# Rounding keys and queries on GpSimd instead of ScalarE from the fourth attention stage on

## The chip, the cores and the metric

The kernel runs on one core of one Trainium2 chip. The metric is the time of one execution on the device in microseconds (us). The engines are TensorE (PE in the rows; PEld is its weight load), VectorE (DVE), ScalarE (ACT), GpSimd (POOL) and SyncE (SP), which issues all the DMAs here. Each engine works through its own queue in order.

## The reference

Attention over 4 batches, 8 heads, 576 positions and 64 dimensions per head, where each query keeps its 32 highest scores; then a mixture of 8 experts whose weights for the rows come from eight rounds of normalising over rows and columns. All in float32.

```python
scores = scale * np.matmul(q, k.transpose(0, 1, 3, 2))
kth = np.partition(scores, -top_k, axis=-1)[..., -top_k:-top_k + 1]
scores = np.where(scores >= kth, scores, -1000000000.0)
attn = np.exp(scores - np.max(scores, axis=-1, keepdims=True))
attn = attn / (np.sum(attn, axis=-1, keepdims=True) + 1e-09)
attn_out = np.matmul(attn, v)                 # -> x, 2304 rows of 512
P = np.exp(x @ w_gate - max)
for _ in range(8):
    P /= P.sum(1, keepdims=True) + 1e-09
    P /= P.sum(0, keepdims=True) + 1e-09
    P *= N / E
for e in range(E):                            # w1: 512 x 1024, w2: 1024 x 512
    out += P[:, e:e + 1] * (np.maximum(x @ w1[e], 0.0) @ w2[e])
```

## The kernel before

**High and low parts.** The matrix products that have to be accurate are made of float32r operands: a value is split into a high part (the value rounded to float32r) and a low part (the value less its high part), and a product is the sum of high by high, high by low and low by high. Three helpers do this: `hi_act` (line 82) rounds on ScalarE, `lo_pool` (line 85) subtracts on GpSimd, `lo_dve` (line 88) subtracts on VectorE.

**Attention.** `STAGES` (line 30) lists seven stages, each one batch with one or both halves of its queries (`phases`), some of them with the last 64 rows as well (`mix`). `attend_stage` runs over the four pairs of heads `hp`; `attend_heads` (line 181) loads and splits what a pair needs. Raw keys and queries come by DMA into the tile `raw` (3 buffers), issued on SyncE. For each of the two heads the keys, 128x576, become `kh` and `kl` (lines 203 and 204); for each half the queries, 128x512, become `qs`, and for the last rows, 128x256, they become `qm` (lines 188 and 189; the low part is put in place in partitions 64 to 127). `scores` (lines 122 and 123) multiplies them on TensorE. ScalarE copies the scores out (`s`, line 128), VectorE finds the 32 highest in four rounds (lines 138 and 141), GpSimd makes a small difference `eb` (line 142), ScalarE weighs (lines 144 and 145), GpSimd adds to the sums `st` (line 171) and multiplies the weights `Et` by the reciprocals (line 175). From the third stage on the weights are turned by a DMA: ScalarE splits them into 16-bit halves (`cross`, line 158), a transposing DMA writes `turned`, and ScalarE puts the halves together into `at` (`whole`, line 165). That last step does not follow its own DMA at once: it waits in the list `turning` and is put behind a later ScalarE instruction (`land`, lines 152 and 147), so that ScalarE has other work while the DMA runs. TensorE then multiplies `at` by the values (line 247).

**The experts.** Beside the attention TensorE works on visits: for an expert and one or two seated blocks of 256 rows, the hidden layer (line 446) and the outputs (line 559). Each visit loads weights as 128x1024 tiles `wr`, which ScalarE rounds to `wh` (line 83, by `hi_act`) and GpSimd turns into `wl` (line 86, by `lo_pool`), six buffers of each. The hidden values are rounded to `hh` on ScalarE (line 514), with `hl` on VectorE (line 515); outputs go through `y` (line 567) to memory. The last four blocks are done at the end in another way (`hidden_pair`, lines 671 to 730), with no attention beside them.

**Order.** The framework plans the order on every engine when the kernel is built, from priorities and its own estimate of each instruction's time; attention has priority over the visits. Within an engine the planned order is fixed at run time, with waits where operands or buffers are not ready. `X` is the dictionary of finished or begun blocks: it has 2 entries in the first stage, 4 in the second, 6 in the third and 9 from the fourth on.

Of the kernel before, what the change touches and what calls it, by code (L numbers as in the profile page):

```python
# [51 lines left out]
def kernel(  # L52
# [11 lines left out]
    nc = tc.nc  # L64
# [16 lines left out]

    def hi_act(dst, src):
        nc.scalar.activation(dst, src, AF.Copy)  # L83

    def lo_pool(dst, src, hi):
        nc.gpsimd.tensor_tensor(dst, src, hi.bitcast(F32), op=OP.subtract)  # L86
# [27 lines left out]
    X = {}  # L114
# [64 lines left out]
    va, vb = slice(0, 64), slice(64, 128)  # L179

    def attend_heads(b, hp, phases, xts, xm):
        lo = lo_dve if (phases, b, hp) == ((0,), 0, 0) else lo_pool

        def load_q(name, o, n, bufs):
            qr = ap_.tile([128, n], F32, name="raw", bufs=RAW)
            nc.sync.dma_start(qr, q[b, hp, :, o:o + n])
            qs = ap_.tile([128, n], F32R, name=name, bufs=bufs)
            hi_act(qs, qr)
            lo(qs[64:128], qr[64:128], qs[64:128])
            return qs  # L190

        def load_phase(ph):
            return load_q("qs", ph * 512, 512, 2)

        if phases:
            qs = load_phase(phases[0])
        ks = []
        for i in range(2):
            kr = ap_.tile([128, S], F32, name="raw", bufs=RAW)
            nc.sync.dma_start(kr, k[b, 2 * hp + i])  # L200
            kh = ap_.tile([128, S], F32R, name="kh", bufs=2)
            kl = ap_.tile([128, S], F32R, name="kl", bufs=2)
            hi_act(kh, kr)
            lo(kl, kr, kh)
            ks.append((kh, kl))
        vr = values[:, hp % 2, :]
        nc.sync.dma_start(vr[:, 0:512], v[b, hp, :, 0:512])
        for i, r in enumerate((va, vb)):
            nc.sync.dma_start(vr[r, 512 + 64 * i:576 + 64 * i], v[b, hp, r, 512:576])
        for ph in phases:  # L210
            if ph != phases[0]:
                qs = load_phase(ph)
            last = ph == phases[-1] and xm is not None
            qm = load_q("qm", 1024, 256, 1) if last else None
            attend_phase(b, hp, qs, qm, ks, vr, xts[ph], xm if last else None)
        if not phases:
            attend_rest(hp, load_q("qm", 1024, 256, 1), ks, vr, xm)
# [34 lines left out]
    def attend_phase(b, hp, qs, qm, ks, vr, xt, xm):  # L252
        nq = 256 if xm is None else 320
        at = ap_.tile([128, 9, 320], F32, name="at", bufs=1)

        def put(blocks, cs, src):
            nc.scalar.activation(at[:, blocks, cs], src, AF.Copy)

        crossed = at if len(X) > 4 else None
        weight_tiles(qs, ks, put, b == 0 or crossed is not None, crossed)  # L260
        if xm is not None:
            def put_rest(rows, blocks, src):
                nc.scalar.activation(at[rows, blocks, 256:320], src, AF.Copy)
            rest_weights(qm, ks, put_rest)
        order = TAIL_FIRST if len(X) > 2 else range(5)

        def weigh():
            av = pst.tile([128, 512], F32, name="pt")
            weigh_values(av, vr, at, nq, order)
            nc.scalar.activation(xt[:, hp, :], av[:, 0:256], AF.Copy)  # L270
            if xm is not None:
                nc.scalar.activation(xm[:, hp, :], av[:, 256:320], AF.Copy)

        if turning:
            turning.append(weigh)
        else:
            weigh()
# [23 lines left out]
    def attend_rest(hp, qm, ks, vr, xm):  # L301
        at = ap_.tile([128, 9, 64], F32, name="tmp", bufs=1)

        def put(rows, blocks, src):
            nc.scalar.activation(at[rows, blocks, :], src, AF.Copy)

        rest_weights(qm, ks, put)
        av = pst.tile([128, 512], F32, name="pt")
        weigh_values(av, vr, at, 64, TAIL_FIRST)
        nc.scalar.activation(xm[:, hp, :], av[:, 0:64], AF.Copy)  # L310

    def attend_stage(b, phases, mix):
# [13 lines left out]
        for hp in range(HP):  # L326
            if (b, phases) == (0, (0,)) and hp in (1, 2):
                with tc.high_priority(offset=-BIG):
                    if hp == 1:
                        first_quarter(xts[0])  # L330
                    else:
                        ready[0] = first_half(xts[0])
            attend_heads(b, hp, phases, xts, xm)
# [45 lines left out]
    def board(blk, seat):  # L379
        pieces = BLOCKS[blk]  # L380
        step = 2 if pieces[0][0] == "t" else 1
        for t in range(0, 2, step):
            x = X[pieces[t]]
            if step == 2:
                x = bass.AP(tensor=x.tensor, offset=x.offset, ap=[list(p) for p in x.ap[:-1]] + [[1, 256]])
            cs = slice(seat.c0 + t * 128, seat.c0 + (t + step) * 128)
            for kk in range(KD):
                hi_act(seat.xh[:, kk, cs], x[:, kk, :])
                lo_dve(seat.xl[:, kk, cs], x[:, kk, :], seat.xh[:, kk, cs])
# [446 lines left out]
```

## Time and profile before

| what | us |
|---|---|
| median of 3 runs (1862.12 to 1863.7) | 1862.87 |
| profiled execution, its own time | 1861.39 |
| its span in the trace | 1859.6 |
| TensorE busy | 1794.2 |
| VectorE busy | 1208.9 |
| ScalarE busy | 1172.1 |
| GpSimd busy | 1047.8 |

How to read the rows below. A line of the stretches gives from:to, its length, then for PE, PEld, DVE, ACT and POOL the busy us and in brackets the number of instructions, then the granted clock of TensorE (1.00 is full speed), the DMA engines' busy share and GB/s. A line of the waits gives engine, line and operation, then whom it waited for: us in total, how many times, the longest. A line of a tile's instructions gives the count, then the shortest, median and longest duration in ns, then the first and last start in us, then the shape; the lines "who: us, times" under it say what ended the idle time of the engine before them. A line of the groups gives the count, then busy us and the mean ns of one, then the idle us before them and who ended it. A line in order of time gives start and duration in us, and in square brackets the idle time before it and who ended that. Matmuls overlap one another in the rows, so TensorE's busy time is not its peak.

### The profile page before, as it was taken

The page shows a single profiled execution, that of the slowest core. Times are in us where ns is not written, and L with a number is a line of the kernel's source. Part 1 is how long each engine was busy: PE and PEld are TensorE (multiplying, and loading weights), DVE is VectorE, ACT ScalarE, POOL GpSimd, SP SyncE. Part 2 cuts the span into 40 slices and gives each one's busy share as a digit, 9 for nine tenths or more (in the row PEclk, how much of TensorE's full clock was granted, in tenths as well). Part 3 has the DMA queues.
Part 4 walks back from the last instruction along what each step waited for, and adds up shares of the span by engine and source line. Part 5 has one row for each costly group of instructions (what it writes and reads, how often), then busy time and mean ns, then how long its engine had stood idle before and what let it go on. Part 6 is the DMA issues. An engine that isn't in the chain of part 4 may idle for free.

```text
span 1859.6 us, 26250 instructions
## 1 busy us (share of the span) xinstructions
PE 1794.2 (96%) x9361; PEld 1484.4 (80%) x9361; DVE 1208.9 (65%) x2235; ACT 1172.1 (63%) x1773; POOL 1047.8 (56%) x827
## 2 busy tenths in 40 slices
PE   4899998999999999999999999999999999999998
PEld 3778787878877878878877788888888888888886
DVE  8989988888888886978965231145555555533433
ACT  5888889898988987898888435433333333333331
POOL 3369755655655547565643948945554455555441
PEclk8999999999999999999999999999999999999999
DMA  4787766666556656565554337523333333311111
GB/s 128 237 286 237 218 173 186 203 169 165 165 144 167 173 135 198 155 160 162 165 134 112 105 131 227 185 85 111 117 110 117 103 102 108 97 62 59 56 35 45
DMA packets 212674, 266.17 MB, mean 143 GB/s; under 512 B 127424, under 2 KB 131648, under 8 KB 212544
## 3 DMA queue, kind: packets, MB, share of 16 engines
q1 hardware_dynamic: 212544, 264.51, 48.0%
q8 instruction: 73, 1.20, 0.3%
q14 instruction: 57, 0.47, 0.1%
HBM read 201.54 MB, written 34.60 MB: 127 GB/s over the span
## 4 chain that ended last, share of the span: by engine, by line
PE 73%; ACT 7%; DVE 6%; issue 5%; DMA 5%; POOL 4%; SPq 0%; ACTq 0%; POOLq 0%; DVEq 0%
PE p L730 19%; PE p L559 15%; PE p L446 14%; PE p L671 9%; PE pc L671 5%; DMA wr<-in_w_dram 3%; PE pt L247 3%; DVE m L138 3%; POOL wl L86 2%; PE pb L671 2%; DVE w L141 2%; PE sp L122 2%; PE sp L123 2%; ACT wh L83 1%; ACT at L165 1%
## 5 line engine op out<-in xcount | busy, mean ns | idle before, releaser
L86 POOL TENSOR_TENSOR wl<-wr,wh 128x1024 fp32r<-128x1024 f32 x280 | 675.1, 2420 | 509.9 <-ACT wh L83 500.1
L83 ACT ACTIVATE wh<-wr 128x1024 fp32r<-128x1024 f32 x280 | 295.1, 1060 | 281.9 <-PE p L671 191.6
L138 DVE MAX8 m<-w 128x8 f32<-128x576 f32 x432 | 321.8, 754 | 6.5
L446 PE MATMUL p<-xh,wh 128*128 128x256 f32 (+1 forms) x800 | 270.3, 338 | 1.5 <-DVE hl L515 1.5
L446 PE MATMUL p<-xh,wl 128*128 128x256 f32 (+1 forms) x800 | 268.4, 336 | 0.0
L446 PE MATMUL p<-xl,wh 128*128 128x256 f32 (+1 forms) x800 | 268.4, 335 | 0.0
L559 PE MATMUL p<-wh,hh 128*128 128x512 f32 x640 | 251.2, 397 | 4.7 <-ACT hh L514 4.5
L559 PE MATMUL p<-wl,hh 128*128 128x512 f32 x640 | 249.2, 392 | 0.0
L559 PE MATMUL p<-wh,hl 128*128 128x512 f32 x640 | 239.5, 391 | 0.0
L141 DVE MATCH_REPLACE8 w<-m,w 128x576 f32<-128x576 f32 x288 | 213.8, 743 | 0.0
L515 DVE SCALAR_TENSOR_TENSOR hl<-p,hh 128x512 fp32r<-128x512 f32 x160 | 109.0, 683 | 148.0 <-ACT hh L514 146.3
L730 PE MATMUL p<-wh,h2h 128*128 128x512 f32 x512 | 199.4, 389 | 1.3 <-ACT h2h L694 0.7
L730 PE MATMUL p<-wl,h2h 128*128 128x512 f32 x512 | 199.2, 389 | 0.0
L730 PE MATMUL p<-wh,h2l 128*128 128x512 f32 x512 | 196.4, 389 | 0.0
L576 DVE SCALAR_TENSOR_TENSOR acc<-p,P,acc 128x512 f32<-128x512 f32 x120 | 89.4, 749 | 160.9 <-PE p L730 160.9
L446 PEld LDWEIGHTS p<-xh,wh 128*128 128x128 f32 x800 | 152.4, 190 | 21.4 <-DVE hl L515 3.1
L446 PEld LDWEIGHTS p<-xh,wl 128*128 128x128 f32 x800 | 152.3, 190 | 15.7 <-issue 0.8
L446 PEld LDWEIGHTS p<-xl,wh 128*128 128x128 f32 x800 | 152.3, 190 | 15.5
L138 DVE MAX8 m<-s 128x8 f32<-128x576 f32 x144 | 108.2, 752 | 76.0 <-ACT s L128 75.3
L559 PEld LDWEIGHTS p<-wh,hh 128*128 128x128 f32 x640 | 120.6, 189 | 30.3 <-ACT hh L514 7.1
L559 PEld LDWEIGHTS p<-wl,hh 128*128 128x128 f32 x640 | 120.7, 189 | 23.0 <-POOL wl L86 0.2
L559 PEld LDWEIGHTS p<-wh,hl 128*128 128x128 f32 x640 | 119.8, 188 | 23.8 <-issue 0.4
(168 smaller groups left out, 3551.8 us busy)
## 6 DMA issues: line engine op xcount, KB each, us to landing
wr<-in_w_dram SPq DMA_DIRECT2D x240, 512.0 KB, 3.5
y<-y SPq DMA_DIRECT2D x160, 256.0 KB, 2.7
raw<-in_k_dram SPq DMA_DIRECT2D x56, 288.0 KB, 3.8
raw<-in_q_dram SPq DMA_DIRECT2D x32, 256.0 KB, 3.7
p<-y SPq DMA_DIRECT2D x32, 256.0 KB, 3.5
wr<-in_w_dram SPq DMA_DIRECT2D x32, 256.0 KB, 4.0
y<-p SPq DMA_DIRECT2D x32, 256.0 KB, 3.8
values<-in_v_dram SPq DMA_DIRECT2D x28, 256.0 KB, 3.1
```

Source lines behind the costliest of these rows:

```text
L83: nc.scalar.activation(dst, src, AF.Copy)
L86: nc.gpsimd.tensor_tensor(dst, src, hi.bitcast(F32), op=OP.subtract)
L122: nc.tensor.matmul(o, qc, kh[:, cs], start=(i == 0), stop=False)
L138: nc.vector.max(m8[:, u, r, :], ws[u] if r else units[u][0])
L141: nc.vector.match_replace(ws[u], m8[:, u, r, :], ws[u] if r else units[u][0], LOWEST)
L247: weighed = nc.tensor.matmul(av[r, 0:n], vr[:, o:o + 64], at[:, block, 0:n], start=(j == order[0]), stop=(j == order[-1]))
L446: nc.tensor.matmul(ps[:, fo, :], a[:, kk, fs], x[:, k0 + kk, cs], start=(i == 0), stop=(i == 3 * nk - 1))
L515: nc.vector.scalar_tensor_tensor(seat.hl[:, ft, cs], src, 0.0, seat.hh[:, ft, cs].bitcast(F32), op0=OP.max, op1=OP.subtract)
L559: nc.tensor.matmul(ps, a[:, ft, ts], m[:, ft % 2, :], start=(i == 0), stop=(i == 3 * NFT - 1))
L576: return nc.vector.scalar_tensor_tensor(ACC[t], y, g, ACC[t], op0=OP.mult, op1=OP.add)
L671: nc.tensor.matmul(ps, w[:, kk, :], x[:, kk, :], start=(fresh and i == 0), stop=(i == 5), skip_group_check=True)
L730: nc.tensor.matmul(ps, a[:, ft, ts], m[:, ft, :], start=(i == 0), stop=(i == 11))
```

## The change

A new helper `hi_pool` rounds on GpSimd with a copy. In `attend_heads` the helper for the high part is chosen by the number of entries in `X`: `hi_act` in the first three stages, `hi_pool` from the fourth stage on. It is used for `qs` and `qm` (in `load_q`) and for `kh`. Who makes the low parts, the loads, the buffers and the late putting together of the halves are the same as before. All other rounding (weights, hidden values, seated rows) stays on ScalarE.

```diff
--- before.py
+++ after.py
@@ -81,6 +81,9 @@
 
     def hi_act(dst, src):
         nc.scalar.activation(dst, src, AF.Copy)
+
+    def hi_pool(dst, src):
+        nc.gpsimd.tensor_copy(dst, src)
 
     def lo_pool(dst, src, hi):
         nc.gpsimd.tensor_tensor(dst, src, hi.bitcast(F32), op=OP.subtract)
@@ -179,13 +182,14 @@
     va, vb = slice(0, 64), slice(64, 128)
 
     def attend_heads(b, hp, phases, xts, xm):
+        hi = hi_pool if len(X) > 6 else hi_act
         lo = lo_dve if (phases, b, hp) == ((0,), 0, 0) else lo_pool
 
         def load_q(name, o, n, bufs):
             qr = ap_.tile([128, n], F32, name="raw", bufs=RAW)
             nc.sync.dma_start(qr, q[b, hp, :, o:o + n])
             qs = ap_.tile([128, n], F32R, name=name, bufs=bufs)
-            hi_act(qs, qr)
+            hi(qs, qr)
             lo(qs[64:128], qr[64:128], qs[64:128])
             return qs
 
@@ -200,7 +204,7 @@
             nc.sync.dma_start(kr, k[b, 2 * hp + i])
             kh = ap_.tile([128, S], F32R, name="kh", bufs=2)
             kl = ap_.tile([128, S], F32R, name="kl", bufs=2)
-            hi_act(kh, kr)
+            hi(kh, kr)
             lo(kl, kr, kh)
             ks.append((kh, kl))
         vr = values[:, hp % 2, :]
```

## Rows read from the trace of the kernel before

**Rows 1.** The page: busy time of the span; the chain that ended last, by engine

```profile
PE 1794.2 (96%) x9361; PEld 1484.4 (80%) x9361; DVE 1208.9 (65%) x2235; ACT 1172.1 (63%) x1773; POOL 1047.8 (56%) x827
PE 73%; ACT 7%; DVE 6%; issue 5%; DMA 5%; POOL 4%; SPq 0%; ACTq 0%; POOLq 0%; DVEq 0%
```

**Rows 2.** Stretches of the span: busy time of each engine, granted clock

```profile
263.00:300.00 37.00, 30.56 (x190) 26.17 (x189) 31.29 (x63) 32.73 (x43) 23.75 (x23) 1.00 0.67 185
300.00:340.00 40.00, 39.16 (x247) 33.12 (x248) 37.58 (x73) 36.26 (x48) 21.91 (x22) 0.92 0.60 166
340.00:420.00 80.00, 76.29 (x505) 66.61 (x504) 70.24 (x140) 72.12 (x110) 44.30 (x41) 0.98 0.69 191
420.00:690.00 270.00, 269.09 (x1418) 219.49 (x1417) 226.63 (x445) 237.09 (x347) 149.16 (x134) 1.00 0.57 155
690.00:705.00 15.00, 15.00 (x82) 11.83 (x81) 7.39 (x14) 11.28 (x21) 14.67 (x12) 1.00 0.86 244
705.00:930.00 225.00, 225.00 (x1255) 183.78 (x1254) 185.27 (x363) 193.79 (x305) 134.30 (x119) 1.00 0.59 165
930.00:1030.00 100.00, 97.84 (x529) 77.72 (x529) 59.41 (x114) 80.87 (x112) 47.34 (x41) 1.00 0.48 131
1140.00:1210.00 70.00, 69.19 (x412) 61.67 (x411) 9.55 (x14) 35.65 (x45) 63.76 (x35) 1.00 0.60 198
1210.00:1859.00 649.00, 643.49 (x2837) 531.99 (x2835) 310.60 (x429) 214.07 (x309) 307.37 (x208) 1.00 0.28 86
```

**Rows 3.** What TensorE waited for, 263.2 to 1030 us

```profile
PE pt L247 <- ACT at L165: 6.2, 1, 6.2
PE sp L122 <- ACT s L128: 3.9, 3, 1.9
PE p L559 <- ACT hh L514: 1.9, 3, 1.2
PE p L446 <- DVE hl L515: 1.1, 1, 1.1
PE pt L362 <- ACT xm L272: 1.0, 1, 1.0
```

**Rows 4.** TensorE in order of time, at its two longest waits

```profile
300.84 4.53 PE L247 MATMUL pt<-at,values 128*64 128x256 f32 x20 [6.22 <-ACT at L165]
379.00 0.40 PE L122 MATMUL sp<-kh,qs 128*128 128x288 f32 x1 [1.95 <-ACT s L128]
```

**Rows 5.** ScalarE in order of time, before those two waits

```profile
290.79 0.68 ACT L83 ACTIVATE kh<-raw 128x576 fp32r<-128x576 f32 x1
291.36 0.62 ACT L83 ACTIVATE qs<-raw 128x512 fp32r<-128x512 f32 x1
372.72 0.63 ACT L83 ACTIVATE qs<-raw 128x512 fp32r<-128x512 f32 x1 [1.67 <-DMA raw<-in_q_dram]
```

**Rows 6.** Tile raw, 263.2 to 1030 us: the roundings, then idle time by its end

```profile
L83 ACT ACTIVATE kh<-raw x32: 667/679/711, 279.9 to 922.9; 128x576 fp32r<-128x576 f32 x32
L83 ACT ACTIVATE qs<-raw x20: 613/632/656, 263.0 to 917.5; 128x512 fp32r<-128x512 f32 x20
L83 ACT ACTIVATE qm<-raw x16: 402/410/449, 271.6 to 924.0; 128x256 fp32r<-128x256 f32 x16
  ACT qs L83: 12.0, 7
  DMA raw<-in_q_dram: 4.6, 4
```

**Rows 7.** GpSimd's groups of instructions, 263.2 to 1030 us

```profile
L86 POOL TENSOR_TENSOR wl<-wr,wh 128x1024 fp32r<-128x1024 f32 x112 | 268.5, 2406 | 154.5 <-ACT wh L83 146.4 <-issue 6.0 <-PE pt L362 0.5
L175 POOL TENSOR_SCALAR Et<-Et,st 128x576 f32<-128x576 f32 x88 | 64.9, 750 | 17.2 <-DVE st L172 16.3 <-PE sp L123 0.3
L86 POOL TENSOR_TENSOR kl<-raw,kh 128x576 fp32r<-128x576 f32 x33 | 46.8, 1434 | 7.0 <-ACT kh L83 6.7
```

**Rows 8.** What ScalarE waited for, 263.2 to 1030 us

```profile
ACT halves L158 <- POOL Et L175: 19.1, 16, 3.0
```

## The prediction

> **What bounds the kernel now.** I read the page first. TensorE is busy for 1794.2 of 1859.6 us and holds 73% of the chain that ended last; ScalarE holds 7%, GpSimd 4% [rows 1]. So work taken off ScalarE is worth nothing as such. It is worth something only where TensorE stood still for ScalarE.
>
> The second view is the table of stretches [rows 2]. The roundings that move start at 263.0 us and the last starts at 924.0 us [rows 6], so the stretches from 263 to 930 us are the ones to look at. In them ScalarE is busy for 32.73 + 36.26 + 72.12 + 237.09 + 11.28 + 193.79 = 583.3 of 667 us, 87.4%, and GpSimd for 388.1 us, 58.2% (added in the same way). TensorE's idle time is 6.44 us up to 300 us, then 0.84, 3.71 and 0.91 us up to 690 us, nothing from 690 to 930 us, and 2.16 us up to 1030 us, 14.1 us together. After 1210 us it is 5.5 us, but no attention runs there, and the change has nothing to move there.
>
> The third view says who ended that idle time: ScalarE in 6.2 + 3.9 + 1.9 + 1.0 = 13.0 us, VectorE in 1.1 us, GpSimd in none [rows 3]. The clock adds to it. The mean granted share is 0.92 from 300 to 340 us, behind the longest wait of 6.22 us [rows 2, 4]. With the levels 2.4 and 1.2 GHz that is some 6.4 us at the lower one, which costs 0.08 x 40 = 3.2 us. From 340 to 420 us (0.98) it is 0.02 x 80 = 1.6 us. What ScalarE can give back from 263 us on is thus at most 13.0 + 4.8 = 17.8 us, under 1% of the time.
>
> **The change part by part.** The threshold is passed in the fourth stage (9 entries in X, against 6 in the third), so four stages change. 32 roundings of keys, 20 of queries and 16 of last rows [rows 6] leave ScalarE. They cost it 32 x 0.679 + 20 x 0.632 + 16 x 0.410 = 21.7 + 12.6 + 6.6 = 40.9 us. ScalarE goes from 583.3 to 542.4 us, 81.3% of the stretch.
>
> **What GpSimd pays.** It runs no copy in the trace of before. The nearest row is line 175, which like the copy reads one tensor: 750 ns for 128x576 [rows 7]. Scaled by columns that is 0.667 us for 512 and 0.333 us for 256, so 24.0 + 13.3 + 5.3 = 42.7 us, and GpSimd goes from 388.1 to 430.8 us, 64.6%. The upper end is line 86 with its two inputs, 1434 ns for 576: 81.6 us, 70.4%. From 1434 ns for 576 and 2406 ns for 1024 columns [rows 7] an instruction's fixed part is 1434 - 576 x 2.17 = 184 ns, and 68 of those, 12.5 us, are the lower end. I take 42.7 us, since line 175 has the same shape and number of inputs. At either end GpSimd keeps over a quarter of the stretch free, so the range of the time doesn't hang on it.
>
> A rule speaks against the change. The Trainium skill (GPSIMD Engine Reference, section 4.1, Engine selection) keeps elementwise work off GpSimd as about half as fast as VectorE with two inputs, though it calls one input roughly line rate. The rows agree on the order: 750 ns with one input, 1434 ns with two. At one column per cycle of the 1.2 GHz that the page states, an estimate for the 68 copies is 27 us. The sum would be the same.
>
> **What hides it.** A low part needs its high part, and GpSimd makes both now, so its waits for ScalarE's query and key roundings (12.0 and 7.0 us [rows 6, 7]) become its own work. The net load on GpSimd is nearer 43 - 19 = 24 us. Behind a rounding stand `wl`, `eb`, `st` and `Et`. For `wl` there is room: GpSimd waited 146.4 us for ScalarE's `wh` before it [rows 7], and TensorE's waits name GpSimd nowhere [rows 3]. The DMAs are not moved; SyncE still issues the raw loads. But `raw` is freed by the low part, later by up to one rounding (0.75 us) where GpSimd was not waiting, and the weight loads stand behind it in SyncE's queue. I cost this at 0, covered by the six weight buffers. If that cover is gone, each such rounding costs up to 0.75 us.
>
> **What the path gains.**
> 1. Ahead of the wait at 300.84 us ScalarE works without a break. Two of its instructions are roundings that move: starts 290.79 and 291.36 us, 0.57 us apart, and the second, 0.62 us less its overlap, some 0.5 us [rows 5]. Gain 1.1 of 6.2 us. What is late next is the same `at`, since the weight roundings stay, so the clock's 3.2 us stay as well.
> 2. At 372.72 us ScalarE waited 1.67 us for a query load and then rounded for 0.63 us, 2.3 us, and TensorE then waited 1.95 us for the scores' copy [rows 4, 5]. On GpSimd that DMA wait holds nobody on ScalarE. Gain 1.95 us.
> 3. The other waits for ScalarE, 13.0 - 6.2 - 1.95 = 4.9 us, I shrink as its free share grows, 12.6% to 18.7%: 4.9 x (1 - 12.6 / 18.7) = 1.6 us, an estimate.
>
> Sum: 1.1 + 1.95 + 1.6 = 4.6 us. Against the profiled execution (span 1859.6 us, own time 1861.4 us) that is 1856.8 us. The median lies 1.5 us above that execution, so the forecast is 1862.9 - 4.6 = 1858.2 us.
>
> The framework plans the order anew from 263 us on. This can shift the waits either way, and the rivals hold what it could do.
>
> **The rivals.**
> - **Covered anyway, 1862.9 us (1860 to 1866).** The planner spends ScalarE's 41 us on issuing other work earlier; TensorE meets its waits elsewhere. For it: from 420 to 930 us TensorE idles under 1 us with ScalarE at 87% [rows 2]. Against it: the second wait above is a queue order that cannot come back in that form.
> - **All of ScalarE's lateness goes, 1862.9 - 17.8 = 1845 us.** For it: 13.0 of 14.1 us name ScalarE [rows 3], and without the 6.2 us wait the clock would not fall. Against it: the chain ahead of that wait holds only 1.1 us of roundings.
> - **Slower: GpSimd's order takes ScalarE's place, 1872 us.** A copy that waits for its load or for TensorE to be done with `kh` now stands in GpSimd's queue ahead of `Et`; `halves` on ScalarE wait for `Et`, `at` waits for both, and TensorE, in order, waits for `at`. ScalarE already waited 16 times for `Et`, 19.1 us in all, 3.0 us at most [rows 8], and GpSimd is busy for 14.67 of 15 us from 690 to 705 us [rows 2]. The price of one such miss is that of the longest wait now: 6.2 + 3.2 us of clock = 9.4 us, so 1872 us, and 1882 us for two. It decides once a rounding makes `Et` later than TensorE's work in hand. Against it: GpSimd still has 35% free, and of the many `at` only one made TensorE wait [rows 3].
> - **It costs GpSimd far more than line 175 says.** This is the upper end, 70.4%, and leads to the third rival rather than to a time of its own.
>
> **How the numbers follow.** Forecast 1858.2 us (1855 to 1861): 0.36. Covered anyway: 0.24. All lateness gone: 0.14. Slower: 0.26. A measurement of this kernel can tell about 0.2%, 3.7 us, from no change, so the bounds are 1859.1 and 1866.6 us. Of the forecast's chance 0.28 lies below 1859.1 us, with 0.14 from the third case: faster 0.42. Same: 0.08 + 0.24 = 0.32. Slower: 0.26. The range goes from 1846 us (all but the full gain) to 1873 us (one miss); two misses and the lowest end are left out, some 0.18. As cases of both signs hold much of the chance: the likeliest one's own range is 1855 to 1861 us.
>
> **What would show it.** In the profile after: 68 copies on GpSimd, near 0.75, 0.67 and 0.33 us; ScalarE's busy time lower by some 41 us and GpSimd's higher by some 43 us; the waits of GpSimd for ScalarE's `kh` and `qs` gone after 263 us; no wait of ScalarE for a query load there; TensorE's idle time from 263 to 1030 us near 9 us instead of 14.1, with the granted clock after the longest wait still dipping. The prediction is wrong if TensorE shows a new wait of over 3 us for `at`, if its waits name GpSimd, or if its idle time falls below 5 us.

## The result and the profile after

The changed kernel takes 1871.93 us (median of 5 runs, 1867.23 to 1872.81) against 1862.12 us in the same comparison. The ratio is 1.0054, 95% interval [1.0041, 1.0067]: 0.5% slower, 7.6 to 12.5 us. The forecast was 1858.2 us. The time lies within the range given, the direction is wrong.

The profiled execution took 1867.23 us with a span of 1865.4 us, against 1861.39 us before, 5.8 us more. Of the page after, the busy time of the engines and the chain that ended last:

```profile
PE 1798.3 (96%) x9361; PEld 1486.3 (80%) x9361; DVE 1214.7 (65%) x2235; ACT 1141.4 (61%) x1705; POOL 1085.4 (58%) x895
PE 77%; DVE 8%; DMA 4%; POOL 4%; ACT 4%; issue 3%; SPq 0%; POOLq 0%; ACTq 0%; DVEq 0%
```

68 instructions have gone from ScalarE (1773 to 1705) and come to GpSimd (827 to 895), as meant [rows 1]. ScalarE is busy 30.7 us less, GpSimd 37.6 us more. The 68 durations that left ScalarE add up to 40.9 us, but its instructions overlap one another in the rows (starts 0.57 us apart, duration 0.68 us [rows 5]), so its busy time falls by less.

Tile `raw` after, from 255 to 1040 us: the copies on GpSimd, then idle time by its end. One copy of queries lies ahead of 263 us. Lines of the changed kernel are 3 or 4 higher than before's.

```profile
L86 POOL CAST kh<-raw x32: 664/671/701, 278.4 to 995.9; 128x576 fp32r<-128x576 f32 x32
L86 POOL CAST qs<-raw x20: 606/615/915, 256.7 to 988.6; 128x512 fp32r<-128x512 f32 x20
L86 POOL CAST qm<-raw x16: 397/407/597, 267.4 to 997.4; 128x256 fp32r<-128x256 f32 x16
  PE sp L125: 16.8, 8
  DMA raw<-in_q_dram: 8.2, 4
```

A copy on GpSimd takes what it took on ScalarE (679, 632 and 410 ns [rows 6]). The last of them starts at 997 us instead of 924 us, so the attention is later. This shows in the last of the top-k instructions on VectorE, in before and then in after (start and duration in us):

```profile
1004.65 0.76 DVE L138 MAX8 m<-w 128x8 f32<-128x576 f32 x1
```
```profile
1072.13 0.75 DVE L141 MAX8 m<-w 128x8 f32<-128x576 f32 x1
```

The stretches of [rows 2], now of after, with one more, 1030 to 1140 us:

```profile
263.00:300.00 37.00, 32.07 (x194) 27.49 (x193) 32.67 (x67) 31.36 (x38) 25.85 (x26) 0.97 0.71 205
300.00:340.00 40.00, 40.00 (x260) 34.31 (x260) 34.71 (x70) 30.38 (x45) 22.36 (x25) 0.99 0.61 159
340.00:420.00 80.00, 75.76 (x512) 65.86 (x512) 62.60 (x120) 62.88 (x93) 49.53 (x47) 0.96 0.61 181
420.00:690.00 270.00, 267.28 (x1370) 216.32 (x1370) 209.69 (x401) 218.19 (x308) 159.72 (x146) 0.99 0.55 155
...
930.00:1030.00 100.00, 99.79 (x495) 80.53 (x494) 79.28 (x152) 84.41 (x119) 60.18 (x57) 1.00 0.56 151
1030.00:1140.00 110.00, 104.22 (x621) 86.46 (x620) 55.40 (x134) 72.72 (x104) 75.41 (x57) 0.97 0.43 122
1140.00:1210.00 70.00, 68.92 (x425) 61.80 (x425) 11.63 (x24) 35.12 (x43) 63.77 (x33) 1.00 0.61 195
```

The same stretch from 1030 to 1140 us of before:

```profile
1030.00:1140.00 110.00, 109.10 (x592) 93.10 (x590) 28.73 (x85) 46.64 (x67) 82.59 (x49) 1.00 0.41 134
```

Up to 1030 us TensorE's idle time is 4.93 + 0 + 4.24 + 2.72 + 0.21 = 12.1 us, against 14.1. From 1030 to 1140 us it is 5.8 us, against 0.9. The clock is read from stretches of 10 us, here all those of after between 263 and 1210 us in which it is below 0.99:

```profile
290.00:300.00 10.00, 6.29 (x35) 5.45 (x36) 8.24 (x18) 9.29 (x10) 8.69 (x6) 0.88 0.95 315
300.00:310.00 10.00, 10.00 (x61) 7.62 (x61) 8.81 (x19) 8.22 (x14) 6.44 (x5) 0.95 0.72 171
350.00:360.00 10.00, 5.88 (x46) 3.08 (x48) 8.19 (x17) 9.94 (x16) 7.73 (x7) 0.66 0.74 251
660.00:670.00 10.00, 7.95 (x39) 5.45 (x40) 4.95 (x10) 7.46 (x12) 4.55 (x7) 0.83 0.72 189
1110.00:1120.00 10.00, 4.79 (x34) 4.51 (x33) 6.31 (x22) 0.91 (x2) 10.00 (x7) 0.84 0.09 29
1120.00:1130.00 10.00, 10.00 (x48) 8.83 (x48) 2.80 (x10) 3.55 (x4) 10.00 (x6) 0.82 0.47 154
```

What the lower of the two levels (1.2 of 2.4 GHz) takes is the missing share times the length: 1.2 + 0.5 + 3.4 + 1.7 = 6.8 us up to 1030 us, against 3.2 + 1.6 = 4.8 us before [rows 2] (5.1 us by stretches of 10 us), and 1.6 + 1.8 = 3.4 us after 1030 us, against nothing. Where the lower clock falls into a wait, both are counted, so the sums below are upper bounds.

So the balance of idle time and clock is 14.1 + 4.8 = 18.9 us before and 12.1 + 6.8 = 18.9 us after up to 1030 us: no gain. From 1030 to 1210 us it is 0.9 + 0.8 = 1.7 us before [rows 2] and 5.8 + 1.1 + 3.4 = 10.3 us after: **8.6 us lost behind the stretch that the forecast looked at**. The medians are 9.8 us apart. The profiled pair is only 5.8 us apart: its execution of after is the shortest of five, 4.7 us under their median, and by 263 us, where only one rounding had moved, it was ahead. TensorE had started 1330 instructions there against 1315 in before; at the mean pace from 263 to 1030 us, 0.18 us for one [rows 2], that is an estimated 2.7 us, so 8.6 - 2.7 = 5.9 us should be left. That stretch in before, then in after:

```profile
0.00:263.00 263.00, 219.45 (x1315) 178.92 (x1316) 242.16 (x501) 211.61 (x377) 158.63 (x151) 0.97 0.69 217
```
```profile
0.00:263.00 263.00, 221.39 (x1330) 180.49 (x1331) 243.98 (x505) 211.91 (x378) 161.72 (x154) 0.99 0.69 218
```

What TensorE waited for in after, the largest entries from 263 to 1030 us and then from 1030 to 1210 us (total, times, longest):

```profile
PE pt L251 <- ACT at L267: 4.2, 1, 4.2
PE p L450 <- DVE hl L519: 3.7, 3, 1.9
PE pt L251 <- ACT at L168: 2.6, 1, 2.6
PE sp L125 <- ACT s L131: 1.2, 1, 1.2
...
PE pt L423 <- DVE cs L421: 2.8, 1, 2.8
PE p L450 <- POOL wl L89: 2.4, 1, 2.4
PE p L563 <- ACT hh L518: 1.1, 1, 1.1
```

The two waits that the forecast named, 6.22 us at 300.84 and 1.95 us at 379.00 [rows 4], are gone. Two others have come at 354 and 662 us. Ahead of the first ScalarE works without a break from 339.38 us, with three weight roundings in front of the `at` that it starts at 350.81 us; ahead of the second it waited 3.83 us for the top-k on VectorE. Neither row has a wait for GpSimd. TensorE in order of time at these and at the two in the later stretch:

```profile
354.12 5.32 PE L251 MATMUL pt<-at,values 128*64 128x320 f32 x20 [4.24 <-ACT at L267]
...
662.05 3.85 PE L251 MATMUL pt<-at,values 128*64 128x256 f32 x20 [2.58 <-ACT at L168]
...
1116.21 0.39 PE L423 MATMUL pt<-cs,ones 128*128 128x8 f32 x2 [2.83 <-DVE cs L421]
1118.98 0.58 PE L450 MATMUL p<-xh,wl 128*128 128x256 f32 x1 [2.38 <-POOL wl L89]
```

The last two lie in what follows the attention. When all rows are there, the experts' weights for the rows are normalised in eight rounds (line 423 is one of their products), and for the blocks done at the end GpSimd prepares the **right factors**: differences of rows (tile `tf`, line 626) and low parts. GpSimd in order of time around the last wait:

```profile
1091.86 2.36 POOL L89 TENSOR_TENSOR wl<-wr,wh 128x1024 fp32r<-128x1024 f32 x1 [5.24 <-ACT wh L83]
1094.17 1.28 POOL L626 TENSOR_TENSOR tf<-xt 128x512 f32<-128x512 f32 x1
...
1115.91 0.72 POOL L626 TENSOR_TENSOR tf<-xt,tf 128x256 f32<-128x256 f32 x1
1116.59 4.67 POOL L89 TENSOR_TENSOR wl<-wr,wh 128x1024 fp32r<-128x1024 f32 x2
```

From 1094.17 to 1116.59 us, 22.4 us, GpSimd works on right factors without a `wl` between. In before the first of them starts at 1031.5 us, beside visits of two blocks, which use each weight for twice the rows. The first products of a visit of a single block start at 1085.4 us, and from 1107.6 us on there are only such visits. They take their `wl` so fast that GpSimd is busy for 63.76 of 70 us from 1140 us on [rows 2]: it has little room for the factors there.

### The profile page after: what moved, and what is told of

It is laid out like the page before. It is cut to its first block, busy times and chain, and to the rows that moved or that the text cites. A ratio compares the mean times of both kernels' runs of the same rounds, so it can differ in the third digit from the quotient of the medians.

```text
span 1865.4 us, 26228 instructions
## 1 busy us (share of the span) xinstructions
PE 1798.3 (96%) x9361; PEld 1486.3 (80%) x9361; DVE 1214.7 (65%) x2235; ACT 1141.4 (61%) x1705; POOL 1085.4 (58%) x895
## 4 chain that ended last, share of the span: by engine, by line
PE 77%; DVE 8%; DMA 4%; POOL 4%; ACT 4%; issue 3%; SPq 0%; POOLq 0%; ACTq 0%; DVEq 0%
PE p L734 19%; PE p L563 17%; PE p L450 16%; PE p L675 9%; PE pc L675 5%; DVE m L141 4%; PE pt L251 4%; DVE w L144 3%; DMA wr<-in_w_dram 3%; POOL wl L89 2%; PE pb L675 2%; PE sp L125 2%; PE sp L126 2%; ACT at L168 1%; ACT wh L83 1%
## 5 line engine op out<-in xcount | busy, mean ns | idle before, releaser
L147 ACT ACTIVATE Et<-s,m 128x576 f32<-128x576 f32 x144 | 111.7, 776 | 55.1 <-DVE m L141 52.1
```

The costliest lines, as they stand in the source:

```text
L147: nc.scalar.activation(Em, s, AF.Prelu, bias=m8[:, u, 3, 7:8], scale=-1.0, alpha=KEPT)
```

## The experiments

The median of before lay between 1860.99 and 1862.38 us in the four comparisons. "First factor" is the first start of line 626 (622 in before).

**The changed kernel again.** No edit.

> The changed kernel once more, for a second trace of it. Its median was 1871.9 us, while the one execution that was profiled took 1867.2 us, the shortest of five. All theories expect 1867 to 1873 us. If the 5 us between them are lost in one place, the new trace shows it: theory A (the attention ends too late, in the stretch of single-block visits) expects it between 1050 and 1150 us; theory B (GpSimd's queue holds Et and eb behind roundings that wait) expects it spread over 300 to 1000 us.

1869.92 us, ratio 1.0051 [1.0037, 1.0065]. From 1090 to 1140 us TensorE is busy for 44.21 us at clock 0.93. The loss is in the same place as in the first execution: the time fits both theories, the place the first one. This profiled execution (1871.08 us) is 3.9 us longer than that one; 2.5 us more are lost from 1140 to 1210 us. The row of the first execution:

```profile
1090.00:1140.00 50.00, 44.22 (x314) 37.84 (x313) 17.22 (x61) 23.30 (x39) 47.94 (x34) 0.93 0.31 105
```

**The right factors on VectorE**, which is busy for 17.22 of those 50 us:

```diff
-                lo_pool(l[:, :, cs], src, h[:, :, cs])
+                lo_dve(l[:, :, cs], src, h[:, :, cs])
...
-            nc.gpsimd.tensor_tensor(dst, a, b, op=OP.subtract)
+            nc.vector.tensor_tensor(dst, a, b, op=OP.subtract)
```

> The changed kernel with the differences and low parts of the right factors (14 subtractions for high-low splits and 8 others, some 30 us of GpSimd right after the attention) on VectorE, which is idle there. The order up to the last scores is that of the changed kernel (3615). Theory A, with the loss at 1110 to 1137 us where GpSimd was busy without a break and TensorE waited for wl: 1862 to 1867 us. Theory B (loss spread over the attention): no change, 1870 to 1873 us.

1861.41 us, 1.0005 [0.9996, 1.0014], 8.5 us less than the changed kernel in the same comparison and just under the first theory's range. The last top-k starts as late as ever (1074.49 us), and so do the factors (1096.3 us), yet the loss is gone. Both waits at 1116 to 1119 us are. The stretch from 1090 to 1140 us:

```profile
1090.00:1140.00 50.00, 49.40 (x366) 42.57 (x365) 28.01 (x66) 31.12 (x46) 31.72 (x13) 1.00 0.47 165
```

**The same edit in the kernel before**, as a control.

> The kernel before with the right factors' subtractions on VectorE, the same edit as in after_factors_dve. The order up to the last scores is that of the kernel before. Theory A: the factors fell beside double-block visits there and cost nothing, so 1859 to 1862 us, within 2 us of the kernel before. If the factors on GpSimd cost as much wherever they stand, it is 1851 to 1855 us, and the 8.5 us that the edit gave in the changed kernel say nothing on lateness.

1864.22 us, 1.0013 [1.0005, 1.0022]. There it gains nothing; it costs a little, 2 us over the range expected. So the 8.5 us are not a gain of the edit as such. They belong to the place where the changed kernel has its factors.

**The last stage late, without the change.** In before, the last stage is planned only when visit 14 is reached and held behind the last matmul of visit 13 (`seen` keeps each visit's last one):

```diff
-        while todo and all(free(i, v) for i in stage_blocks[todo[0]]):
-            with tc.high_priority(offset=BIG):
+        while todo and all(free(i, v) for i in stage_blocks[todo[0]]) and (len(todo) > 1 or v >= 14):
+            held = ExitStack()
+            if len(todo) == 1:
+                held.enter_context(tc.issue_after(seen[v - 1].ins))
+            with held, tc.high_priority(offset=BIG):
```

> The kernel before, all roundings on ScalarE, with the last attention stage held back in TensorE's order until the last matmul of visit 13. Its normalising rounds then stand at matmuls 3748 to 3959 of the planned order, against 3493 to 3820 in the kernel before and 3725 to 3980 in the changed kernel. Theory A (what costs is the late end of the attention, whose right factors meet the single-block visits on GpSimd): 1867 to 1874 us, lost between 1080 and 1150 us with GpSimd's subtractions in a row. Theory B (GpSimd's queue with the roundings in it): 1859 to 1863 us, since no rounding is on GpSimd.

1860.97 us, 0.9993 [0.9984, 1.0001]. My theory expected a loss and missed. The last top-k is at 1057.08 us, the first factor at 1085.5 us, 9 us ahead of the changed kernel's. From 1090 to 1140 us:

```profile
1090.00:1140.00 50.00, 48.24 (x326) 42.22 (x325) 20.02 (x69) 22.38 (x32) 48.73 (x32) 1.00 0.41 132
```

TensorE stands still for 1.8 us and the clock holds. So an end 52 us later costs nothing by itself here; the table below shows from when on it does.

**The last stage on ScalarE.** The stage with an empty tuple of phases, which rounds only keys and last rows, gets its old helper:

```diff
-        hi = hi_pool if len(X) > 6 else hi_act
+        hi = hi_pool if len(X) > 6 and phases else hi_act
```

> The changed kernel with the roundings of the last stage alone (the one with an empty tuple of phases, four heads' rows) back on ScalarE; those of the three stages ahead of it stay on GpSimd. Theory A (the copies and lows of the last stage queue behind one another on GpSimd, and this is what made its pairs of heads take 16 us instead of 10): the last top-k starts within 20 us of before's 1004.7 us, the right factors run ahead of 1060 us, and the time is 1858 to 1864 us. Theory B (the attention is late by the planned order of the stages ahead of it, which already were 37 us late; which engine rounds in the last stage does not matter): the last top-k starts after 1035 us, the right factors again run beside visits of one block, and the time is 1866 to 1872 us.

1862.59 us, 1.0008 [0.9995, 1.0022]. It fell between: the last top-k is at 1049.96 us (the second theory's side), the time and the clean stretch from 1090 to 1140 us are the first one's, though its factors start later than the first theory had it. (That stage is the sixth of seven, not the last, as the expectation calls it.) The first factor is at 1077.0 us, 17 us earlier than in the changed kernel, and from 1090 to 1140 us:

```profile
1090.00:1140.00 50.00, 50.00 (x305) 44.74 (x304) 21.05 (x70) 23.39 (x30) 48.13 (x26) 1.00 0.50 168
```

With those 12 copies back on ScalarE, 22 of the 67.5 us by which the attention ends later are gone. In the changed kernel the copies of this stage wait for TensorE to be done with the keys two heads before, and the low parts wait behind them:

```profile
777.90 1.28 POOL L86 CAST kh<-raw 128x576 fp32r<-128x576 f32 x2 [6.67 <-PE sp L125]
```

**A later threshold**, `len(X) > 14` in place of 6. It moves one stage alone, the last: 8 copies of keys, 8 of queries and 4 of last rows.

> The changed kernel with the threshold at more than 14 entries in X instead of more than 6, so that only the last stages round on GpSimd. In its planned order the normalising rounds stand among the visits of two blocks again, 200 instructions ahead of where the changed kernel has them. Theory A (what the change costs is lost where the right factors and the normalising meet the visits of one block): no such loss between 1090 and 1140 us, TensorE busy for over 48 of these 50 us, and the time is 1858 to 1866 us. Theory B (what costs is GpSimd's queue in the stages with moved roundings themselves, the last stage above all): the time is 1867 to 1873 us, with TensorE's new waits ahead of 1030 us.

1860.53 us, 0.9994 [0.9985, 1.0004]. The last top-k is at 1007.46 us, the first factor at 1034.0 us, and from 1090 to 1140 us TensorE has no gap, as the first theory had it:

```profile
1090.00:1140.00 50.00, 50.00 (x315) 45.35 (x314) 9.09 (x26) 22.79 (x28) 33.92 (x15) 1.00 0.53 176
```

**Keys alone, queries alone.** `hi_act` for the queries and last rows, or for the keys, in the changed kernel:

```diff
-            hi(qs, qr)
+            hi_act(qs, qr)
```
```diff
-            hi(kh, kr)
+            hi_act(kh, kr)
```

> Only the 32 key roundings move to GpSimd, the 36 of queries stay on ScalarE. The planned order has 3408 matmuls ahead of the last scores, a third of the delay from 3298 to 3615. Theory A: a third of the loss or less, 1862 to 1866 us. Theory B: the waits of GpSimd for TensorE to be done with kh (16.8 and 3.1 us in the trace of the changed kernel) are all those of keys, so most of the loss stays: 1868 to 1872 us.

> Only the 36 roundings of queries and last rows move to GpSimd, the 32 of keys stay on ScalarE. The planned order has 3223 matmuls ahead of the last scores, fewer than the 3298 of the kernel before, so the attention ends earlier. Theory A: no loss at the end, 1856 to 1862 us. Theory B, in the form that the trace of the tensor_scalar run shows at 364 to 376 us (a query rounding waits for its load in GpSimd's queue, and Et, halves and TensorE wait behind it): 1864 to 1870 us.

Keys alone: 1857.50 us, 0.9987 [0.9977, 0.9998], a little faster, with the first factor at 1047.6 us. Up to 1030 us this kernel has what the forecast looked for: from 263 us on idle time and missing clock are 8.0 + 3.4 = 11.4 us, against 14.1 + 5.1 = 19.2 us in before, and 16.6 + 8.5 = 25.1 us for queries alone (all by stretches of 10 us). It then loses some of it among its factors, where GpSimd is busy without a break (the waits there name `hl` and line 421 on VectorE):

```profile
1070.00:1080.00 10.00, 6.96 (x30) 5.40 (x31) 5.24 (x19) 4.02 (x5) 10.00 (x6) 1.00 0.30 105
```

Queries alone: 1874.04 us, 1.0066 [1.0053, 1.0079], with the last top-k at 995.33 us, earlier than before's. Both theories missed both times: for keys alone they gave too high a time, for queries alone too low a one (the second one 1864 to 1870 us). The loss of queries alone has another place and cause. TensorE there, at its two longest waits, and ScalarE at the first and last instruction ahead of the first wait:

```profile
356.21 5.43 PE L251 MATMUL pt<-at,values 128*64 128x320 f32 x20 [4.64 <-ACT at L168]
...
421.32 0.80 PE L563 MATMUL p<-wh,hh 128*128 128x512 f32 x1 [2.85 <-ACT hh L518]
...
341.14 2.13 ACT L161 ACTIVATE halves<-Et 128x2304 uint16<-128x2304 uint16 x1 [3.14 <-DMA turned<-halves]
...
353.78 2.38 ACT L168 ACTIVATE at<-turned 128x2304 uint16<-128x2304 uint16 x1
```

ScalarE waits 3.14 us for the transposing DMA and then runs without a break from 341.14 us to the `at` of 353.78 us, with three weight roundings in that row, and no rounding of a query holds it up. So it is the planned row on ScalarE that is late, not GpSimd's queue. This wait for `at`, of 4.2 to 5.2 us between 354 and 358 us, stands in five traces in which these roundings of queries had moved (the two of the changed kernel, factors on VectorE, sixth stage on ScalarE, queries alone), and not in those of keys alone. The traces of the other form of the copy, the fourth buffer and the other planned order, all below and with them moved, lack it, so it takes the order too. The two waits shown have a stretch of the lower clock beside them (0.73 from 350 to 360 us, 0.69 from 420 to 430 us).

**The copy in another form.** The same values by a multiplication, which the planner estimates otherwise:

```diff
-        nc.gpsimd.tensor_copy(dst, src)
+        nc.gpsimd.tensor_scalar(dst, src, 1.0, 1.0, op0=OP.mult, op1=OP.mult)
```

> The same 68 roundings stay on GpSimd, written as a multiplication by 1.0 twice instead of a copy. The planned order of TensorE then has 3297 visit and product matmuls ahead of the last scores, against 3298 in the kernel before and 3615 in the changed kernel. Theory A (the loss is in the order: the attention is planned later and its end meets the single-block visits): 1859 to 1864 us, last top-k search near 1005 us instead of 1072 us. Theory B (the loss is GpSimd's queue at run time, roundings that wait for TensorE or a load hold the rest): 1869 to 1874 us, since GpSimd has the same roundings with the same waits, each a little longer (0.75 us, the row of line 175).

1872.91 us, 1.0070 [1.0054, 1.0086]. On the chip the form takes as long (medians 678, 622 and 408 ns against 671, 615 and 407). Yet the last top-k starts at 1015.22 us instead of 1072.13, and TensorE has no gap from 1090 to 1140 us. So most of the lateness is the order planned, not time that the copies take. The time is as bad, as the second theory had it, for a loss ahead of 1030 us: 20.9 + 11.9 = 32.8 us of idle time and missing clock from 263 us on, against 18.9 us in the changed kernel. GpSimd, ScalarE and TensorE there, around 370 us:

```profile
364.08 0.62 POOL L86 TENSOR_SCALAR qs<-raw 128x512 fp32r<-128x512 f32 x1 [0.89 <-DMA raw<-in_q_dram]
364.67 2.41 POOL L89 TENSOR_TENSOR wl<-wr,wh 128x1024 fp32r<-128x1024 f32 x1
367.15 1.29 POOL L89 TENSOR_TENSOR qs<-raw,qs 64x512 fp32r<-64x512 f32 x1
368.55 1.48 POOL L178 TENSOR_SCALAR Et<-Et,st 128x576 f32<-128x576 f32 x2
...
370.06 2.12 ACT L161 ACTIVATE halves<-Et 128x2304 uint16<-128x2304 uint16 x1 [2.85 <-POOL Et L178]
...
375.75 0.80 PE L563 MATMUL p<-wh,hh 128*128 128x512 f32 x1 [3.73 <-ACT hh L518]
```

This is the third rival as the prediction had it: a copy that waits for its load, `Et` behind it, `halves` waiting for `Et`, and TensorE for what stands behind them on ScalarE. Here it exists. In the changed kernel it doesn't: ScalarE waits 5.3 us for `Et` in all and 1.4 us at most, against 19.1 and 3.0 us before [rows 8].

**Another planned order for both kernels.** Each visit is wrapped in a priority offset of zero, which adds no instruction and changes the order alone:

```diff
-        visit(turn, [blk for blk in BOARD if BOARD[blk] <= turn < BOARD[blk] + E])
+        with tc.high_priority(offset=0):
+            visit(turn, [blk for blk in BOARD if BOARD[blk] <= turn < BOARD[blk] + E])
```

> The kernel before with every visit wrapped in a priority block of offset 0. No work, engine or buffer changes; only the planned order does (3110 matmuls ahead of the last scores instead of 3298). Theory C (the order that the planner happens to make is worth several us, whatever the edit): anywhere from 1854 to 1872 us, more than 3 us from the kernel before. Theory A (only a late end of the attention costs): 1859 to 1863 us, since it ends early.

> The changed kernel with the same wrapping. Its attention ends at 3384 matmuls, and the normalising rounds stand at 3584 to 3812, nearly where they stand in the kernel before, so the right factors fall beside double-block visits again. Theory A: the change is worth what was forecast without its loss at the end, 4 to 6 us less than before_replanned. Theory C: the difference from before_replanned has either sign, up to 10 us.

1920.23 us (1.0306 [1.0292, 1.0319]) without the change and 1888.28 us (1.0133 [1.0118, 1.0148]) with it: in this order the change is worth 32 us. Every theory missed both: none gave over 1872 us without the change, or a difference over 10 us. The stretch from 263 to 420 us without it, then with it:

```profile
263.00:420.00 157.00, 140.18 (x883) 120.12 (x884) 130.62 (x259) 135.64 (x197) 84.33 (x82) 0.92 0.67 179
```
```profile
263.00:420.00 157.00, 146.62 (x960) 127.64 (x961) 135.79 (x267) 130.75 (x184) 96.86 (x99) 0.96 0.66 179
```

Here TensorE waits more for ScalarE (16.8 us idle in this stretch without the change, 10.4 with it, and clock 0.92 against 0.96; ScalarE ended most of it in both), and taking work off ScalarE goes with a gain. That the gain comes from this and not from the order alone is not shown.

**A fourth buffer for `raw`**, in both kernels (`RAW` 4 in place of 3), against a copy that waits for a free buffer.

> The kernel before with four buffers for raw keys and queries instead of three, so that loads are issued earlier. The attention ends at 3211 matmuls. Theory A: 1859 to 1862 us. Theory C: anywhere from 1854 to 1872 us.

> The changed kernel with four buffers for raw keys and queries. Fewer roundings wait for a load on GpSimd, but the attention still ends late (3566 matmuls, normalising rounds at 3762 to 3980). Theory A: still a loss at the end, 6 to 12 us over before_raw4. Theory B (roundings that wait for loads hold GpSimd's queue): the loss goes, within 2 us of before_raw4. Theory C: either sign.

1865.41 us (1.0019 [1.0007, 1.0030]) and 1871.03 us (1.0044 [1.0030, 1.0058]). Without the change the time is above the first theory's range and within that of a third, by which any order can be worth several us. The difference stays, 5.6 us, just under what the first theory gave it and far from the second's. With the change the first factor is at 1092.6 us, and from 1090 to 1140 us:

```profile
1090.00:1140.00 50.00, 47.67 (x336) 41.04 (x333) 16.71 (x57) 23.24 (x39) 49.53 (x35) 0.97 0.32 105
```

Without the change its first factor starts at 1007.3 us, and TensorE is busy for all 50 us. With it, more is lost behind this stretch, at a wait of 3.0 us for `hh` at 1170 us: from 1030 to 1210 us 8.8 us in all, against 2.1 us. No wait there names `wl`.

**Keys alone with the right factors on VectorE**, both edits from above.

> Key roundings on GpSimd and the right factors' subtractions on VectorE. The keys alone gave 1857.5 us with some 7 us still lost between 1050 and 1200 us. Theory A: 1852 to 1857 us, faster than both kernels. If those 7 us are not the factors': 1857 to 1859 us.

1855.33 us, 0.9963 [0.9951, 0.9976]: faster than both kernels, by 7 us against before, and in the first theory's range. From 1030 to 1210 us 1.9 us are lost, against 4.1 us for keys alone (some 7 us by the expectation).

Put side by side, in the order of the first factor; the loss is idle time plus missing clock from 1030 to 1210 us, by stretches of 10 us, so that the factors lie inside it for every kernel:

| kernel | first factor, us | on | loss, us |
|---|---|---|---|
| before | 1031.5 | GpSimd | 1.7 |
| last stage alone | 1034.0 | GpSimd | 2.0 |
| keys alone | 1047.6 | GpSimd | 4.1 |
| sixth stage on ScalarE | 1077.0 | GpSimd | 0.4 |
| before, last stage held | 1085.5 | GpSimd | 2.8 |
| after, fourth buffer | 1092.6 | GpSimd | 5.4 + 3.4 = 8.8 |
| after | 1094.2 | GpSimd | 6.9 + 3.4 = 10.3 |
| after, factors on VectorE | 1096.3 | VectorE | 0.6 |

The loss does not grow evenly with lateness. It is small up to 1085.5 us, large from 1092.6 us on, and gone when GpSimd has no factors. Each line is one execution; the second one of after lost 12.8 us.

## Why the prediction was wrong

**What leaves ScalarE and what GpSimd pays** held. The copies took 671, 615 and 407 ns where 750, 667 and 333 ns were taken from line 175, together 21.5 + 12.3 + 6.5 = 40.3 us instead of 42.7. GpSimd is busy 37.6 us more where some 43 were expected, ScalarE 30.7 us less where 41 were: the durations were right, but added up they leave out the overlap. By the first and the last, 320 columns cost 264 ns, 0.83 ns each, and the fixed part is 196 ns. The Trainium skill (GPSIMD Engine Reference, section 4.1, Engine selection) calls one input on GpSimd roughly line-rate and two inputs about half as fast as VectorE. The trace agrees that the second input costs: 671 ns with one input, 1440 ns with two (`kl`).

**Steps 1 and 2** held for the waits they named: both are gone, the first one whole and not by 1.1 us, with 1.5 + 1.2 + 1.9 us of shorter waits between 290 and 298 us in its place.

**Step 3**, the other waits shrink by 1.6 us, failed, and so did the clock's part. Waits of 4.24 us at 354 us and 2.58 us at 662 us are new and bring 3.4 and 1.7 us at the lower clock. TensorE's idle time from 263 to 1030 us is 12.1 us where 9 were expected, and the balance with the clock is zero, which is the first rival's amount. It is not that nothing was there to gain: keys alone gave 19.2 - 11.4 = 7.8 us up to 1030 us, and queries alone lost 5.9 us. With the factors on VectorE in both kernels (1.0005 with the change, 1.0013 without) the change is worth nothing that can be measured.

**The step that set the direction** was the term for what comes behind 1030 us, which was put at nothing without a reason. The opening adds up TensorE's idle time to 1030 us and goes on after 1210 us ("no attention runs there, and the change has nothing to move there"); the 180 us between have no term, and of the order planned anew it says only that "This can shift the waits either way". I gave no price to the attention ending later and didn't ask what follows it and on which engine. It ended 67.5 us later, the right factors moved from visits of two blocks to where those of one begin, and 8.6 us were lost there. That this is the place is shown by the factors on VectorE (-8.5 us), with the control in before (no gain), and by the table above. That all of it is GpSimd's lack of room is not shown: the first wait there, 2.83 us, names the normalising on VectorE, and the edit that moves the factors also plans anew what follows the attention.

**GpSimd "keeps over a quarter of the stretch free"** was right for 263 to 930 us and not for the place that decided: 47.94 of 50 us busy from 1090 to 1140 us. (Of the 7.0 us taken as GpSimd's waits for `kh`, 6.7 name it [rows 7]; that changes nothing here.) An average over the stretch of the moved instructions says nothing on what those instructions push into another.

**The third rival** gave the right time, 1872 us, by another mechanism in another place. Its waits were seen with the other form of the copy at 364 to 376 us, not in the changed kernel. Two of the signs of being wrong did appear: a new wait of over 3 us for `at` (4.24 us at 354 us), and a wait of TensorE that names GpSimd, 2.4 us for `wl`, which the text had not connected with any case.

**What stays open.** How the 67.5 us of lateness divide. The sixth stage's copies back on ScalarE took 22 us away, another form of the copy, equal in time on the chip, took 57 us; both also change the planned order, so the two don't add. Most of it is thus the order, and why the planner makes it so was not followed. Nor was it settled why ScalarE gets such a row of work ahead of `at` at 354 us once the queries' roundings have moved, or why the wait for line 421 went with the factors, though VectorE had more to do.

## What to carry to other kernels

Where a framework plans the order from estimated times, an edit is also a new order, and its sign can come from that: a copy of equal duration in another form moved the end of the attention by 57 us, and in another order of the same kernel the change was worth -32 us instead of +10. An edit of several parts can hide a gain: here, each in its own planned order, the part on the keys gained where the part on the queries lost. So when work is moved, look past the stretch in which it runs: when does the stage now end, what waits for that end, which engine does it run on, and is that engine free there? A control, the same rescue applied to the kernel before, tells a cause from a gain of its own.

## What the runs showed that I had not expected

A wait of TensorE of 2 to 5 us mostly costs more than its length. Behind the wait of 4.24 us at 354 us the clock's missing share was 3.4 us, behind the 2.58 us at 662 us it was 1.7 us, and behind the two of 2.83 and 2.38 us at 1116 to 1119 us 3.4 us. Not always: the wait of 1.95 us at 379 us in before [rows 4] has no stretch of the lower clock beside it. The order alone can cost 3%: the priority offset of zero, with the same instructions, took the kernel before from 1861 to 1920 us.
